# Linear attention and two feed-forward layers in one launch: stores put ahead of loads in the DMA queue, and an attention tile's transpose one step further from its normalisation

## The chip, the cores and the metric

The kernel runs on one core of a Trainium2 chip. The metric is the device time of one execution in microseconds (us); the result quoted for a kernel is the median of several runs. All data is float32; matrix products are made from a high and a low part of each factor, three matmuls for each product.

## The reference

Per batch (8) and head (8), over 576 positions of 64 elements, then over 4608 tokens of 512 elements:

```python
kv  = einsum('bhsd,bhse->bhde', k, v)
o   = einsum('bhsd,bhde->bhse', q, kv)
x   = o / sqrt(mean(o*o, -1) + 1e-6) * g_norm      # laid out as 4608 x 512
h   = x @ w_in1                                    # 512 -> 2048
y   = (h * sigmoid(1.702*h)) @ w_out1              # 2048 -> 512
h2  = y @ w_in2
out = (s * maximum(h2, 0)**2 + b) @ w_out2
```

## The kernel before, in words

**First layer: 144 steps.** Tokens are cut into nine blocks of 512, the 2048 inner features into sixteen groups of 128. A step `n` is one block and one group: `mm1(n)` (L375, 12 matmuls with 512 columns) makes `h`, `act_g`, `act_h` and `act_l` make its activation and its two parts on ScalarE (ACT) and VectorE (DVE), and `mm2(n-2)` (L404, 12 matmuls) adds the group of two steps before to the four sums of the block. Steps 0 to 31 go over blocks 0 and 1 together; from step 32 on, each block has sixteen steps. The loop at L855 writes the order out by hand, and every engine takes its instructions in this order. In each step it runs named slots: `splith`, `mm1`, `norm`, `pe`, `mm2(n-2)`, the copies of a finished block's sums (`y_out`), `act`, `r`, `turn`, `xh`, `xl`, `raw`, `load`, and then two calls of `make`.

**Attention rides along.** For block v (3 and up) with first step n0 = 16(v-1), `kv_at` puts one pair of heads of batch v into each of the steps n0 to n0+3 (`kv_pair` on PE, L223); `load_kv` loads the pair p+2 in the step of pair p, two steps ahead of its use, into buffers `kt` and `vt`. A block has four attention tiles. `tile_at(i, n, n_norm, n_turn)` puts the product `att_u` (PE) with its square `att_sq` (ACT) and row sums `att_r` (DVE, then GpSimd) into step n, the normalisation `att_norm` (DVE, L291) into `n_norm`, and the transposes `att_turn` (PE, L297) with their copies `att_xh`, `att_xl` into `n_turn`. `load_q` loads a tile's q four steps before n.

**Work for the second layer** is done beside the steps 35 to 145, as generators: each call of `make(True)` or `make(False)` advances the first generator of its list to the next `yield`, and goes on to the next generator if that one ends. `prep_in` and `prep_out` split the second layer's weights into parts (an ACT copy L176 or L184, a DVE subtraction L177 or L185) in the one buffer `wst`, which is stored to DRAM. `factors(s)` reads back the first layer's result (`yf`, L342 and L345), adds the parts of blocks 0 and 1 (L349), forms seven combinations (L356 to L359) and stores each as a high and a low part from one of two buffers `xo` (L363, L364).

**One DMA queue.** Every transfer is issued by SyncE (SP), in the order of the program. An instruction that waits holds up all behind it. `move` (L83) issues stores and loads alike; `load_wo` refills, six steps ahead, a ring of eight weight buffers, and waits for the `mm2` that used the buffer last. `load_w` (L108) loads raw weights and waits for the conversion of an earlier one (L134).

**Second layer: 40 pairs.** For each of five couples of blocks and eight pairs of feature groups, seven `product`s (L467) with a Strassen-like scheme are each followed by `after` (L516, on ACT and DVE) and by one or two `units` of the output product (L555). `make(False)` runs what is left of `factors`.

Of the kernel before, what the change touches and what calls it, by code (L numbers as in the profile page):

```python
# [24 lines left out]
TT = BT // P  # L25
# [18 lines left out]
def tile_attn_moe_moe2(  # L44
# [26 lines left out]
    def new(tag, shape=(P, BT), dtype=F32, name=None):  # L71

        return sb.tile(list(shape), dtype, tag=tag, name=name or tag)

    def rot(tag, n, shape=(P, BT), dtype=F32, name=None):

        turns[tag] = turns.get(tag, -1) + 1
        return new(f"{tag}{turns[tag] % n}", shape, dtype, name or tag)

    def move(dst, src):  # L80

        raw = [x.bitcast(F32) if x.dtype == F32R else x for x in (dst, src)]
        nc.sync.dma_start(out=raw[0], in_=raw[1])  # L83
# [94 lines left out]
        move(dst, t)  # L178

    def prep_out(f):  # L180
        w = w_raw.pop((1, 1, f))
        wo_dram[1, f] = dp.tile([P, 2, DM], F32, name=f"wo1_{f}")
        t = new("wst", (P, 2, DM), F32R)
        nc.scalar.copy(t[:, 0, :], w)  # L184
        nc.vector.tensor_tensor(out=t[:, 1, :], in0=w, in1=t[:, 0, :].bitcast(F32), op=ALU.subtract)  # L185
        move(wo_dram[1, f], t)
        yield

    def prep_in(p):
        a, b = (w_raw.pop((0, 1, f)).rearrange("p (h e) -> p h e", h=2) for f in (2 * p, 2 * p + 1))  # L190
# [138 lines left out]
    def factors(s):  # L329


        js = [j for j in (2 * s, 2 * s + 1) if j < NB]
        m = BT * len(js) // 2
        x_dram[s] = [dp.tile([P, 2, 2, m], F32, name=f"x{s}_{i}") for i in range(7)]
        tt = nc.vector.tensor_tensor
        for c in range(2):
            got = {}
            for kk in range(2):
                for n, j in enumerate(js):
                    t = got[kk, n] = new(f"yf{2 * kk + n}")  # L340
                    first, *more = y_dram[j].values()
                    nc.sync.dma_start(out=t, in_=first[2 * kk + c])  # L342
                    others = [new(f"yf{4 + e}") for e, _ in enumerate(more)]
                    for o, part in zip(others, more):
                        nc.sync.dma_start(out=o, in_=part[2 * kk + c])  # L345
                    if others:
                        yield
                    for o in others:
                        tt(out=t, in0=t, in1=o, op=ALU.add)  # L349
            if len(js) == 2:  # L350
                b11, b12, b21, b22 = (got[x] for x in ((0, 0), (0, 1), (1, 0), (1, 1)))
            else:
                (b11, b12), (b21, b22) = ((got[x, 0][:, 0:m], got[x, 0][:, m:]) for x in range(2))
            t1, t2, t4 = (new(f"yf{e}")[:, 0:m] for e in (4, 5, 6))
            yield
            tt(out=t1, in0=b12, in1=b11, op=ALU.subtract)  # L356
            tt(out=t2, in0=b22, in1=t1, op=ALU.subtract)
            tt(out=b12, in0=b22, in1=b12, op=ALU.subtract)
            tt(out=t4, in0=b21, in1=t2, op=ALU.subtract)  # L359
            for i, x in enumerate((b11, b21, t2, t1, b12, b22, t4)):  # L360
                yield
                o = rot("xo", 2, (P, 2, m), F32R)
                nc.scalar.copy(o[:, 0, :], x)  # L363
                tt(out=o[:, 1, :], in0=x, in1=o[:, 0, :].bitcast(F32), op=ALU.subtract)  # L364
                move(x_dram[s][i][:, c], o)
# [9 lines left out]
    def mm1(n, t0=0, t1=BT):  # L375
        v_, f = steps[n][:2]
        wh, wl = w_in[f]
        xh, xl = xT[v_]
        if t0 == 0:
            h_t[n] = bank(f"h{n % 2}", "h")  # L380
        o = h_t[n][:, t0:t1]
        for c in range(KD):
            cs = slice(c * P, (c + 1) * P)
            nc.tensor.matmul(o, wh[:, cs], xh[:, c, t0:t1], start=(c == 0), stop=False)  # L384
            nc.tensor.matmul(o, wl[:, cs], xh[:, c, t0:t1], start=False, stop=False)  # L385
            nc.tensor.matmul(o, wh[:, cs], xl[:, c, t0:t1], start=False, stop=(c == KD - 1))  # L386
# [11 lines left out]
    def act_l(n):  # L398
        gl = gl_t[n] = rot("gl", 2, dtype=F32R)
        nc.vector.tensor_tensor(out=gl, in0=g_t.pop(n), in1=gh_t[n].bitcast(F32), op=ALU.subtract)  # L400
# [213 lines left out]
    def at(n, slot, fn, *args):  # L614
        beside.setdefault((n, slot), []).append((fn, args))

    def run(n, slot):
        for fn, args in beside.pop((n, slot), ()):
            fn(*args)

    def tile_at(i, n, n_norm, n_turn, slot="turn"):

        at(n, "pe", att_u, i)
        at(n, "act", att_sq, i)
        at(n, "r", att_r, i)
        at(n_norm, "norm", att_norm, i)
        at(n_turn, slot, att_turn, i)
        early = "0" if slot == "pe" else ""
        at(n_turn, "xh" + early, att_xh, i)
        at(n_turn, "xl" + early, att_xl, i)  # L630

    def kv_at(bb, p, n):
        at(n, "pe", kv_pair, bb, p)
        if p + 2 < NP:
            at(n, "load", load_kv, bb, p + 2)
        if p == NP - 1:
            at(n, "act", kv_out, bb)
            if bb + 1 < B:
                next_kv(bb + 1, n)
# [19 lines left out]
    n0 = begin[1, CUTS[-2]]  # L659
# [9 lines left out]
    for v_ in range(3, NB):  # L669
        n0 = begin[v_ - 1, 0]  # L670
        if v_ < B:
            for p in range(NP):
                kv_at(v_, p, n0 + p)
        for t in range(TT):
            n = n0 + 4 + 3 * t
            at(n - 4, "load", load_q, v_ * TT + t)
            tile_at(v_ * TT + t, n, n + 1, n + 1)


    def need(w):  # L680
# [36 lines left out]
    with tc.manual_schedule():  # L717
# [131 lines left out]
        def make(weights):  # L849

            got = made[weights]
            while got and next(got[0], got) is got:
                got.popleft()

        for n in range(2, len(steps) + 2):  # L855
            conv = to_f32(*convs.pop(n)) if n in convs else iter(())
            for fn, *args in todo.pop(n, ()):
                made[fn is not factors].append(fn(*args))
            run(n, "splith")
            next(conv, None)  # L860
            if n <= len(steps):
                act_l(n - 1)
            next(conv, None)
            run(n, "splitl")
            next(conv, None)
            if n < len(steps):
                if n > 2:
                    mm1(n)
                act_g(n)
                act_h(n)  # L870
            else:
                for i in (0, 1) if n == len(steps) else (2, 3):
                    product(0, i)
                    after(0, i)
            run(n, "norm")
            run(n, "pe")
            next(conv, None)
            run(n, "xh0")
            run(n, "xl0")
            mm2(n - 2)  # L880
            y_out(n - 2, 0)
            y_out(n - 2, 1)
            run(n, "act")
            run(n, "r")
            next(conv, None)
            y_out(n - 2, 2)
            y_out(n - 2, 3)
            run(n, "turn")
            run(n, "xh")
            run(n, "xl")  # L890
            run(n, "raw")
            run(n, "load")
            make(True)
            make(False)
            if n == NB * KF - 15:
                load_half(0)
                load_half(1)
            if NB * KF - KF < n < NB * KF - 1 and n % 2:
                load_x(0, (n - NB * KF + KF) // 2)
            if n == len(steps):  # L900
                load_half(2)
            if n >= len(steps) - 6 and n % 2:
                load_wo2()
                load_wo2()
# [3 lines left out]
        for P_, (cp, p) in enumerate(pairs):  # L908
            for i in range(4 if P_ == 0 else 0, 7):
                product(P_, i)  # L910
                after(P_, i)
                if i == 2 and P_:
                    running.append(units(P_ - 1))
                for _ in range(2 if i == 6 else 1):
                    while running and next(running[0], StopIteration) is StopIteration:
                        running.pop(0)
                make(False)
                if i == 3 and P_:
                    load_half(2 * P_ + 3)
                if i == 6:  # L920
                    load_half(2 * P_ + 4)
                if cp + 1 < len(couples):
                    if p == 0 and i in (5, 6):
                        load_x(cp + 1, i - 5)
                    if p == KF // 2 - 1 and i < 5:
                        load_x(cp + 1, i + 2)
# [56 lines left out]
```

## Time and profile before

| | us |
|---|---|
| median of 3 runs | 1708.98 (1707.16 to 1713.73) |
| profiled execution, its own time | 1713.6 |
| span of the profiled execution | 1711.8 |
| PE busy | 1639.8 (96%) |
| DVE busy | 911.6 (53%) |
| ACT busy | 667.6 (39%) |

The span is the time from the first to the last instruction of the profile; the execution's own time is 1.8 us longer. A wait is the time in which an engine stood idle before an instruction, put down to the work whose end released it. The 16 DMA engines moved 375.76 MB, 220 GB/s over the span.

### The profile page before, as it was taken

The page shows a single profiled execution, that of the slowest core. Times are in us where ns is not written, and L with a number is a line of the kernel's source. Part 1 is how long each engine was busy: PE and PEld are TensorE (multiplying, and loading weights), DVE is VectorE, ACT ScalarE, POOL GpSimd, SP SyncE. Part 2 cuts the span into 40 slices and gives each one's busy share as a digit, 9 for nine tenths or more (in the row PEclk, how much of TensorE's full clock was granted, in tenths as well). Part 3 has the DMA queues.
Part 4 walks back from the last instruction along what each step waited for, and adds up shares of the span by engine and source line. Part 5 has one row for each costly group of instructions (what it writes and reads, how often), then busy time and mean ns, then how long its engine had stood idle before and what let it go on. Part 6 is the DMA issues. An engine that isn't in the chain of part 4 may idle for free.

```text
span 1711.8 us, 21305 instructions
## 1 busy us (share of the span) xinstructions
PE 1639.8 (96%) x7996; PEld 1354.3 (79%) x7996; DVE 911.6 (53%) x1512; ACT 667.6 (39%) x1161; POOL 75.1 (4%) x52
## 2 busy tenths in 40 slices
PE   8899999989979999999999799999999999999998
PEld 6687887767867878777888688888888888888887
DVE  5876637565446544665544455554454454555443
ACT  4565633434334433443333343333334333333333
POOL 3200101000000000000000000000000000000000
PEclk9999999989989999999999999999999999999999
DMA  6566757686566845767478964684377447644773
GB/s 222 168 220 202 265 203 273 244 294 222 197 227 241 311 161 185 265 226 265 148 273 299 319 234 135 224 286 142 135 262 252 139 148 263 208 136 148 245 277 118
DMA packets 125239, 375.76 MB, mean 220 GB/s; under 512 B 14416, under 2 KB 18000, under 8 KB 119632
## 3 DMA queue, kind: packets, MB, share of 16 engines
q1 hardware_dynamic: 125136, 374.40, 63.1%
q8 instruction: 63, 1.03, 0.2%
q14 instruction: 40, 0.33, 0.1%
HBM read 284.69 MB, written 89.65 MB: 219 GB/s over the span
## 4 chain that ended last, share of the span: by engine, by line
PE 77%; DMA 10%; DVE 7%; ACT 2%; issue 2%; SPq 1%; POOL 0%; ACTq 0%; DVEq 0%; POOLq 0%
PE h L384 6%; PE h L385 6%; PE h L386 6%; PE acc L413 5%; PE acc L414 5%; PE acc L415 5%; DMA wi<-wst 4%; PE sum L575 4%; PE sum L576 4%; PE sum L577 4%; PE A L480 4%; PE A L482 4%; PE A L481 4%; PE z L575 3%; PE z L576 3%; PE z L577 3%
## 5 line engine op out<-in xcount | busy, mean ns | idle before, releaser
L384 PE MATMUL h<-xh,wih 128*128 128x512 f32 (+1 forms) x580 | 234.2, 404 | 0.0
L413 PE MATMUL acc<-gh,wo 128*128 128x512 f32 x576 | 230.6, 400 | 3.4 <-DVE xl L318 3.4
L385 PE MATMUL h<-xh,wil 128*128 128x512 f32 (+1 forms) x580 | 230.5, 397 | 0.0
L386 PE MATMUL h<-xl,wih 128*128 128x512 f32 (+1 forms) x580 | 230.2, 397 | 0.2 <-DVE xl L318 0.2
L414 PE MATMUL acc<-gh,wo 128*128 128x512 f32 x576 | 225.7, 392 | 1.3 <-DVE wo L150 1.3
L415 PE MATMUL acc<-gl,wo 128*128 128x512 f32 x576 | 225.7, 392 | 1.0 <-DVE gl L400 1.0
L391 ACT ACTIVATE g<-h 128x512 f32<-128x512 f32 x144 | 86.0, 597 | 254.0 <-PE h L386 253.7
L392 DVE TENSOR_TENSOR g<-g,h 128x512 f32<-128x512 f32 x144 | 98.6, 685 | 148.2 <-ACT g L391 148.0
L396 ACT CAST gh<-g 128x512 fp32r<-128x512 f32 x144 | 89.5, 621 | 172.3 <-DVE g L392 172.3
L386 PEld LDWEIGHTS h<-xl,wih 128*128 128x128 f32 x580 | 112.3, 194 | 24.5 <-DVE xl L318 0.4
L385 PEld LDWEIGHTS h<-xh,wil 128*128 128x128 f32 x580 | 112.7, 194 | 22.6
L384 PEld LDWEIGHTS h<-xh,wih 128*128 128x128 f32 x580 | 112.5, 194 | 22.6
L413 PEld LDWEIGHTS acc<-gh,wo 128*128 128x128 f32 x576 | 108.9, 189 | 26.8 <-DVE xl L318 3.6
L415 PEld LDWEIGHTS acc<-gl,wo 128*128 128x128 f32 x576 | 108.7, 189 | 24.4 <-DVE gl L400 1.4
L414 PEld LDWEIGHTS acc<-gh,wo 128*128 128x128 f32 x576 | 108.9, 189 | 23.1 <-DVE wo L150 2.0
L400 DVE TENSOR_TENSOR gl<-g,gh 128x512 fp32r<-128x512 f32 x144 | 99.9, 694 | 26.4 <-PE acc L415 24.6
L287 POOL TENSOR_TENSOR r<-ms,mhalf 128x8 f32<-128x8 f32 x36 | 65.4, 1823 | 752.6 <-DVE ms L286 752.6
L480 PE MATMUL A<-wih,xl 128*128 128x512 f32 (+1 forms) x212 | 79.0, 373 | 7.6 <-ACT gh L544 7.6
L524 DVE TENSOR_TENSOR wst<-B,wst 128x512 f32<-128x512 f32 (+1 forms) x40 | 25.5, 638 | 99.2 <-PE B L482 99.2
L481 PE MATMUL A<-wih,xl 128*128 128x512 f32 (+1 forms) x212 | 78.3, 369 | 0.0
L482 PE MATMUL A<-wil,xl 128*128 128x512 f32 (+1 forms) x212 | 78.2, 369 | 0.0
L585 DVE TENSOR_TENSOR g<-z,g 128x512 f32<-128x512 f32 x56 | 38.7, 691 | 55.8 <-PE z L577 55.5
(236 smaller groups left out, 3146.2 us busy)
## 6 DMA issues: line engine op xcount, KB each, us to landing
wo<-wo SPq DMA_DIRECT2D x208, 512.0 KB, 4.6
x<-xo SPq DMA_DIRECT2D x56, 512.0 KB, 5.2
xl<-wi SPq DMA_DIRECT2D x26, 1024.0 KB, 5.3
xl<-wi SPq DMA_DIRECT2D x27, 768.0 KB, 4.4
wraw<-in_w_in SPq DMA_DIRECT2D x32, 512.0 KB, 3.6
wraw<-in_w_out SPq DMA_DIRECT2D x32, 512.0 KB, 3.5
y<-ev SPq DMA_DIRECT2D x60, 256.0 KB, 2.9
yf<-y SPq DMA_DIRECT2D x60, 256.0 KB, 5.2
```

The lines of the kernel that those rows point to most:

```text
L384: nc.tensor.matmul(o, wh[:, cs], xh[:, c, t0:t1], start=(c == 0), stop=False)
L385: nc.tensor.matmul(o, wl[:, cs], xh[:, c, t0:t1], start=False, stop=False)
L386: nc.tensor.matmul(o, wh[:, cs], xl[:, c, t0:t1], start=False, stop=(c == KD - 1))
L413: nc.tensor.matmul(o, wh[:, ds_], gh, start=(f == lo), stop=False)
L414: nc.tensor.matmul(o, wl[:, ds_], gh, start=False, stop=False)
L415: nc.tensor.matmul(o, wh[:, ds_], gl, start=False, stop=(f == hi - 1))
L480: nc.tensor.matmul(o, wh, xh, start=(c == 0 and not more), stop=False, skip_group_check=more)
L481: nc.tensor.matmul(o, wl, xh, start=False, stop=False, skip_group_check=more)
L482: nc.tensor.matmul(o, wh, xl, start=False, stop=(c == 1), skip_group_check=more)
L575: nc.tensor.matmul(o, gh[:, cs], wh, start=begins, stop=False)
L576: nc.tensor.matmul(o, gh[:, cs], wl, start=False, stop=False)
L577: nc.tensor.matmul(o, gl[:, cs], wh, start=False, stop=ends)
```

## The change

`prep_out` yields before its work and not behind it. `factors` yields once more after it has added the parts of blocks 0 and 1. For blocks 3 to 8 an attention tile's product and normalisation come one step earlier (n0+3+3t and n0+4+3t) and its transposes stay where they were (n0+5+3t); its q is loaded one step earlier too. In the steps of the first layer `make` runs ahead of the slots `raw` and `load`, so that the stores and the reads of `prep_in`, `prep_out` and `factors` come ahead of that step's loads in SP's queue. In the second layer `make(False)` runs after products 1 and 4 of a pair and not after each of the seven.

```diff
     def prep_out(f):
+        yield
         w = w_raw.pop((1, 1, f))
...
         move(wo_dram[1, f], t)
-        yield
...
                     for o in others:
                         tt(out=t, in0=t, in1=o, op=ALU.add)
+                    if others:
+                        yield
...
         for t in range(TT):
-            n = n0 + 4 + 3 * t
+            n = n0 + 3 + 3 * t
             at(n - 4, "load", load_q, v_ * TT + t)
-            tile_at(v_ * TT + t, n, n + 1, n + 1)
+            tile_at(v_ * TT + t, n, n + 1, n + 2)
...
             run(n, "xl")
+
+            make(True)
+            make(False)
             run(n, "raw")
             run(n, "load")
-            make(True)
-            make(False)
...
-                make(False)
+                if i in (1, 4):
+                    make(False)
```

## Rows read from the trace of the kernel before

**Rows 1.** The page: TensorE clock granted in 40 slices of the span, in tenths.

```profile
PEclk9999999989989999999999999999999999999999
```

**Rows 2.** Busy time by stage: window, length, busy time (x instructions) of each engine, clock, DMA.

```profile
256.00:944.00 688.00, 650.57 (x3202) 533.23 (x3201) 369.38 (x634) 253.38 (x445) 43.95 (x24) 0.97 0.68 240
944.00:1003.00 59.00, 49.12 (x195) 38.92 (x194) 29.56 (x52) 22.21 (x41) 0.00 (x0) 0.91 0.84 294
1003.00:1626.00 623.00, 623.00 (x2778) 517.10 (x2777) 318.29 (x472) 224.08 (x364) 0.00 (x0) 1.00 0.57 196
```

**Rows 3.** Waits of PE from 256 to 944 us: total, times, longest.

```profile
PE xtp L297 <- ACT gh L396: 21.2, 4, 10.9
PE xtp L297 <- DVE xn L291: 15.2, 7, 3.4
```

**Rows 4.** The longest wait of PE from 944 to 1003 us.

```profile
PE A L480 <- ACT gh L544: 5.5, 1, 5.5
```

**Rows 5.** Busy time of four steps: a stalled transposing step and its next, two unstalled ones.

```profile
474.12:491.34 17.22, 6.33 (x30) 5.09 (x28) 6.29 (x11) 2.84 (x5) 1.95 (x1) 0.81 0.88 305
491.34:498.64 7.30, 7.30 (x26) 5.88 (x25) 4.51 (x8) 4.05 (x7) 0.00 (x0) 0.74 0.17 72
504.99:510.79 5.80, 5.80 (x30) 4.82 (x28) 2.52 (x5) 1.22 (x2) 1.95 (x1) 1.00 0.69 247
510.79:516.36 5.57, 5.57 (x27) 4.59 (x26) 4.50 (x8) 4.04 (x7) 0.00 (x0) 1.00 0.51 188
```

**Rows 6.** Timeline of DVE: start, length, instruction, idle time before it and its releaser.

```profile
485.17 0.69 DVE L356 TENSOR_TENSOR yf<-yf,yf 128x512 f32<-128x512 f32 x1 [7.93 <-DMA yf<-y]
...
488.57 0.68 DVE L400 TENSOR_TENSOR gl<-g,gh 128x512 fp32r<-128x512 f32 x1
...
489.77 0.68 DVE L291 TENSOR_TENSOR xn<-u,r 128x512 f32<-128x512 f32 x1
```

**Rows 7.** Timeline of SP's queue in the same stretch.

```profile
469.95 0.32 SPq L83 DMA_DIRECT2D wo<-wst  x1
473.31 0.33 SPq L108 DMA_DIRECT2D wraw<-in_w_in  x1
...
477.89 2.33 SPq L342 DMA_DIRECT2D yf<-y  x4
```

**Rows 8.** Timeline of PE: another stalled transpose.

```profile
376.83 1.08 PE L297 MATMUL xtp<-ident,xn 128*128 128x128 f32 x4 [7.75 <-ACT gh L396]
```

**Rows 9.** Timeline of SP's queue before it.

```profile
364.09 0.33 SPq L83 DMA_DIRECT2D wo<-wo  x1
364.70 0.33 SPq L83 DMA_DIRECT2D wi<-wst  x1
```

**Rows 10.** Timeline of ACT in the same stretch.

```profile
371.01 0.62 ACT L176 CAST wst<-wc 128x512 fp32r<-128x512 f32 x1 [3.04 <-DMA wi<-wst]
```

**Rows 11.** Timeline of ACT at the start of the second layer.

```profile
963.11 0.62 ACT L363 CAST xo<-yf 128x512 fp32r<-128x512 f32 x1 [2.40 <-DMA x<-xo]
...
972.23 0.41 ACT L363 CAST xo<-yf 128x256 fp32r<-128x256 f32 x1 [4.39 <-DMA yf<-y]
```

**Rows 12.** The tile wst, 250 to 900 us: from the issue of a store to its landing.

```profile
DMA to landing us min/median/max: 2.0/3.7/8.3
```

**Rows 13.** Timeline of SP's queue: the load of batch 4's last pair of v.

```profile
348.77 0.50 SPq L218 DMA_DIRECT2D vt<-in_v  x1
```

**Rows 14.** The tile vt, 345 to 360 us: from issue to landing.

```profile
DMA to landing us min/median/max: 4.6/4.6/4.6
```

**Rows 15.** Timeline of PE: the product that uses it.

```profile
353.54 0.69 PE L237 MATMUL kvps<-vt,kt 128*64 128x64 f32 x16
```

**Rows 16.** The same for batch 5: SP's queue, 453 to 458 us.

```profile
456.76 0.60 SPq L218 DMA_DIRECT2D vt<-in_v  x1
```

**Rows 17.** The tile vt, 455 to 465 us: from issue to landing.

```profile
DMA to landing us min/median/max: 6.2/6.2/6.2
```

**Rows 18.** Timeline of PE: the product that uses that load.

```profile
464.18 0.69 PE L237 MATMUL kvps<-vt,kt 128*64 128x64 f32 x16
```

## The prediction

> **What bounds the kernel now.** The first view is the page. TensorE (PE) is busy 96% of the span, and the granted clock stands at nine tenths or more in all slices but two [rows 1]. So nothing can be won on PE's work, which the change leaves as it is; what can be won is PE's idle time and the time in which its clock is down. The busy time by stage says where that lies. From 1003 to 1626 us PE has no gap and full clock: 2778 matmuls in 623 us, 4.459 a microsecond. From 256 to 944 us it is busy 650.57 of 688.00 us at a mean clock of 0.97, and from 944 to 1003 us 49.12 of 59.00 us at 0.91 [rows 2]. The waits of PE name the causes. In the first stretch 21.2 + 15.2 us of the 37.4 us idle stand before the transposes of attention tiles (L297); a single wait of 1.0 us is somewhere else [rows 3]. In the second stretch products wait for ACT to empty a sum, 5.5 us the first and longest time [rows 4].
>
> **What a stall costs beside itself.** A step whose transposes wait, from the start of its mm1 to that of the next, took 17.22 us and the step behind it 7.30 us; an unstalled couple took 5.80 and 5.57 us [rows 5]. The excess is 13.15 us, of which 10.89 us is PE's idle time (17.22 less 6.33), so 2.26 us is matmuls at a low clock: the granted clock was 0.74 in the step behind the stall, a mixture of the levels 1.2 and 2.4 GHz, after PE had stood still. Eight of the twelve waits in this stretch are longer than 1.5 us (10.9 us the longest [rows 3]), and each is followed by such a slow spell; behind the four shorter ones the timeline has none. 8 x 2.26 = 18.1 us. The mean clock of 0.97 over 688 us says 20.6 us, so the two agree roughly [rows 2].
>
> **The ceiling of the gain.** From 256 to 944 us: 37.4 + 18.1 = 55.5 us. From 944 to 1003 us: at 4.459 a microsecond 59.00 us hold 263.1 matmuls, and 195 were made, so 68.1 x 0.224 us = 15.3 us are lost, idle time and clock together. In all 70.8 us. The profiled execution's own time was 1713.6 us, so with all of this gone it is 1642.8 us. Before 256 and behind 1003 us the change touches nothing that PE waits for. The median shown, 1709.0 us, is 4.6 us below this execution; I don't take that off, because what differs between executions is most likely the stalls, and without them both end at the same place.
>
> **Two steps between product and transpose.** Where the largest stall ended, DVE had stood 7.93 us for a read of yf; then came the four combinations, the low part gl at 488.57 us, and the normalisation at 489.77 us, 0.68 us long, for which the transposes waited [rows 6]. With the transposes a step later PE goes on with the next mm1: twelve matmuls, 2.7 us. Then it comes to the mm2 that needs this very gl, ready at 489.25 us. The normalisation ended at 490.45 us and PE had then waited 10.9 us [rows 3], from 479.6 us on; it would stop again at 482.3 us and wait 7.0 us. So this part alone takes 3.9 us from a stall: the waits for DVE of at most 3.4 us [rows 3] go entirely, that of 10.9 us becomes 7.0 us, and one of 7.75 us [rows 8] 3.8 us. The other two of the four put down to ACT share 2.55 us (21.2 - 10.9 - 7.75) and go too. The moved instructions cost nothing: product, square and row sums fall into the step before, where they lie beside the step's 24 matmuls; in each block's fourth step they share PE with a kv_pair, and the same matmuls are missing one step later. The product's bank comes free in the step behind its own, as before; the transposes use the other one of the two banks. The q load moves one step earlier with its product and stays four steps ahead.
>
> **Stores and reads ahead of loads.** For the 10.9 us: the yf reads were issued at 477.89 us, behind a raw weight load that had waited for DVE until 473.31 us and eight other loads. The last store before them was issued at 469.95 us [rows 7]. Behind that store alone, the reads go out near 470.3 us, 7.6 us earlier; DVE's 7.93 us become about 0.3 us, and what was left of this stall goes. For the 7.75 us: a wst store was issued at 364.70 us behind the ring's refill at 364.09 us, which waits for PE's mm2 [rows 9]; the next ACT copy into the single buffer waited 3.04 us for its landing [rows 10], and DVE, the combinations and the normalisation came behind it. With the store ahead, most of the 3.04 us goes and so do the remaining 3.8 us. The extra yields (eight, in factors(0) alone; sixteen prep_outs a step later) move work of 0.4 to 0.7 us a piece into steps where DVE has room: it is busy 369 of 688 us [rows 2]. They lengthen factors(0) from 24 to 32 calls, which still end where factors(1) begins; nothing reads the result before step 129.
>
> What is put behind the stores is late by what they take: ring refills and raw loads have six steps in hand, some 33 us, and can bear that. The kv loads have two steps, and are the tight place. The last pair of batch 4 is issued at 348.77 us [rows 13], lands 4.6 us later [rows 14], and its product starts at 353.54 us [rows 15]: 0.17 us in hand. For batch 5 it is 456.76 us [rows 16] plus 6.2 us [rows 17] against 464.18 us [rows 18]: 1.2 us. Ahead of the first there is now an xo store, ahead of the second a wst store and an xo store, 512 KB each; at the 305 GB/s of the fullest step shown [rows 5] that is 1.7 us a store. Lower bound 0: the yf reads that filled the queue just before go away from there, and DVE is no longer late. Upper bound, with 1.4 us more for SP's wait on DVE (two operations of 0.7 us) and batch 6 taken as batch 5: 2.9 + 3.6 + 3.6 = 10.1 us, and three slow spells, 6.8 us: 16.9 us. I take 3 us, nearer the lower end, because the queue is emptier there than before.
>
> **make(False) at two of seven products.** ACT stood 2.40 us for the landing of an xo store and 4.39 us for a yf read [rows 11], and the copies that free PE's banks were queued behind it [rows 4]. Now a call comes every three or four products, some 9 us apart, longer than either needs; the seventeen calls left end some nine pairs in, and the fifth couple needs them in pair 31. Of the 15.3 us I leave 2 us standing.
>
> **Sum.** 1642.8 + 3 (kv loads) + 2 (second layer's start) + 2 (DVE and ACT late now and then in the first) = 1650 us.
>
> **Rivals.** Kv loads late: the stores' bytes and SP's wait at the upper bound in three blocks, 1650 - 3 + 16.9 = 1664 us. For it speak margins of 0.17 and 1.2 us, against it the reads that leave the queue. The Trainium skill (DMA: Bandwidth & Descriptors, Queues, rings and completion order) says that each DMA engine takes the descriptors of one queue in ring order, so that a load behind two stores starts behind their bytes; by that this rival holds in full, and no run here shows yet how much of it does.
>
> The low part takes the transpose's place: the queue's part brings nothing, gl stays late, and PE waits 7.0 + 3.8 us with two slow spells of 2.26 us, 15.3 us instead of 2: 1663 us. Against it: the rows name SP's order as the cause of both.
>
> The second layer's start stays as it is, since ACT is late there for another reason: 1650 - 2 + 15.3 = 1663 us.
>
> The other side: wst is one buffer, and now five users follow each other step by step, eight times. One turn is 0.62 us (ACT), 0.69 us (DVE), 0.33 us (issue) and the landing, 3.7 us in the median and 8.3 us at most [rows 6, 7, 10, 12]: 5.3 us against a step of about 5.7 us. If every landing took 8.3 us, a turn would be 9.9 us, ACT would fall 4.2 x 5 = 21.2 us behind in each group, and less one step of slack that is 15.5 x 8 = 124 us: 1774 us. It decides from the landing at which 8 x (5 x (L + 1.64 - 5.7) - 5.7) reaches the 63.6 us of the gain, L = 6.8 us; the median is far from that.
>
> **How the numbers follow.** Forecast 0.60, kv loads 0.16, gl 0.13, second layer's start 0.05, wst 0.03, and 0.03 that losses I don't see eat the gain up. A measurement of this kernel tells changes over about 0.5% (8.5 us) from none. The forecast and the first three rivals are faster by 45 us or more: 0.94; no change 0.03; slower 0.03. The range goes from just below the ceiling's 1642.8 us to the three rivals at 1663 and 1664 us, which it holds in part.
>
> **What would show it.** Right: from 256 to 944 us no wait of PE before L297 over 1 us, granted clock 1.00, DVE's wait for yf before L356 and ACT's for wst near 0, xo stores and yf reads ahead of the refill in SP's queue; from 944 us on no wait before L480. Wrong: waits before L237 (kv loads), before L415 (gl), or ACT at L176 and L184 behind the landing of wst in every step.

## The result and the profile after

| | us |
|---|---|
| before, median | 1710.68 (1707.16 to 1713.73) |
| after, median | 1656.53 (1655.56 to 1658.53) |
| ratio | 0.9686, 95% interval 0.9663 to 0.9709 |
| profiled execution of after: own time, span | 1656.05, 1654.2 |
| predicted | 1650 (1642 to 1664) |

The page of the kernel after, clock granted in 40 slices, which answers to [rows 1]:

```profile
PEclk9899999999999999999999999999999999999999
```

The busy time by stage; the columns are those of [rows 2]. The second layer's first product stands at 892.88 us here and stood at 943.67 us before, so the stages are cut there:

```profile
256.00:892.80 636.80, 634.76 (x3210) 524.11 (x3209) 368.65 (x632) 252.83 (x445) 43.63 (x23) 1.00 0.73 259
892.80:950.00 57.20, 52.64 (x218) 42.62 (x217) 29.79 (x47) 21.57 (x38) 0.00 (x0) 0.94 0.79 284
...
1003.00:1570.00 567.00, 567.00 (x2533) 470.67 (x2532) 289.93 (x432) 204.10 (x333) 0.00 (x0) 1.00 0.59 203
```

In the first layer PE now misses 2.04 us of 636.80 where it missed 37.43 us of 688.00 us before [rows 2], and its granted clock is 1.00. At the second layer's start 4.56 us are still idle and the clock is 0.94. The waits of PE of the kernel after, 256 to 1000 us, where [rows 3, 4] stood before. The line numbers of this kernel have moved by one to three: L343 and L359 to L362 here are L342 and L356 to L359 of before, L403 is L400, L483 is L480:

```profile
PE A L483 <- ACT gh L547: 2.5, 1, 2.5
PE z L578 <- DVE g L585: 2.1, 1, 2.1
PE kvps L237 <- DMA vt<-in_v: 2.0, 2, 1.4
```

No line of a transpose (L297) is left. Two of the three lines are new: kv products that wait for their load, and a product of the output units (z) that waits for DVE; before, one such product waited 0.4 us, just behind this stretch.

SP's queue of the kernel after, in the step in which factors(1) begins, as in [rows 7]:

```profile
450.05 0.32 SPq L83 DMA_DIRECT2D wo<-wst  x1
450.65 0.32 SPq L83 DMA_DIRECT2D x<-xo  x1
451.02 2.93 SPq L343 DMA_DIRECT2D yf<-y  x4
454.00 0.43 SPq L108 DMA_DIRECT2D wraw<-in_w_in  x1
```

The reads of yf stand behind two stores only, and the raw load and the eight others behind them. DVE in the same stretch, as in [rows 6]:

```profile
453.18 0.68 DVE L291 TENSOR_TENSOR xn<-u,r 128x512 f32<-128x512 f32 x1
455.87 0.69 DVE L359 TENSOR_TENSOR yf<-yf,yf 128x512 f32<-128x512 f32 x1 [2.01 <-DMA yf<-y]
458.28 0.69 DVE L360 TENSOR_TENSOR yf<-yf,yf 128x512 f32<-128x512 f32 x1 [1.71 <-DMA yf<-y]
...
460.09 0.68 DVE L403 TENSOR_TENSOR gl<-g,gh 128x512 fp32r<-128x512 f32 x1
```

The wait of 7.93 us has become 2.01 + 1.71 us, and the normalisation of this tile (L291) now stands ahead of it. ACT's waits for the buffer wst, 256 to 900 us, are one line, of 28.2 + 24.6 us in two before:

```profile
ACT wst L176 <- DMA wi<-wst: 11.1, 4, 3.6
```

### The profile page after: what moved, and what is told of

The parts are those of the page before. It is cut to its first block, busy times and chain, and to the rows that moved or that the text cites. A ratio compares the mean times of both kernels' runs of the same rounds, so it can differ in the third digit from the quotient of the medians.

```text
span 1654.2 us, 21293 instructions
## 1 busy us (share of the span) xinstructions
PE 1621.3 (98%) x7996; PEld 1343.6 (81%) x7996; DVE 911.6 (55%) x1512; ACT 665.8 (40%) x1161; POOL 75.6 (5%) x52
## 4 chain that ended last, share of the span: by engine, by line
PE 93%; DMA 3%; DVE 2%; ACT 1%; issue 1%; SPq 0%; ACTq 0%; DVEq 0%
PE acc L416 8%; PE acc L418 8%; PE acc L417 8%; PE h L387 8%; PE h L389 8%; PE h L388 8%; PE sum L578 4%; PE sum L579 4%; PE sum L580 4%; PE A L483 4%; PE A L484 4%; PE A L485 4%; PE z L578 3%; PE z L579 3%; PE z L580 3%; PE D L485 2%
## 5 line engine op out<-in xcount | busy, mean ns | idle before, releaser
L387 PE MATMUL h<-xh,wih 128*128 128x512 f32 (+1 forms) x580 | 228.6, 394 | 0.0
L389 PE MATMUL h<-xl,wih 128*128 128x512 f32 (+1 forms) x580 | 225.7, 389 | 0.2 <-DVE xl L318 0.2
L388 PE MATMUL h<-xh,wil 128*128 128x512 f32 (+1 forms) x580 | 225.6, 389 | 0.0
L403 DVE TENSOR_TENSOR gl<-g,gh 128x512 fp32r<-128x512 f32 x144 | 99.9, 694 | 28.5 <-PE acc L418 26.8
L483 PE MATMUL A<-wih,xl 128*128 128x512 f32 (+1 forms) x212 | 79.3, 374 | 4.6 <-ACT gh L547 4.6
```

What stands on the lines that cost most here:

```text
L483: nc.tensor.matmul(o, wh, xh, start=(c == 0 and not more), stop=False, skip_group_check=more)
```

## Experiments

The ratios are to the kernel before on the same chip. The medians of before were 1709.85 us for the first four and 1709.97 us for the last four.

**Spacing alone.**

```diff
-            n = n0 + 4 + 3 * t
+            n = n0 + 3 + 3 * t
...
-            tile_at(v_ * TT + t, n, n + 1, n + 1)
+            tile_at(v_ * TT + t, n, n + 1, n + 2)
```

> The kernel before with the attention tiles' new spacing alone (product and normalisation a step earlier, transposes where they were). My theory: SP's queue makes DVE and ACT late, and the spacing only gives one step of slack; no wait before the transposes L297, but PE waits for the low part gl in mm2 for about 7.0 and 3.8 us; idle time of PE from 256 us to the first product of the second layer about 11 us (37.4 before), with two slow spells; gain about 40 us, ratio 0.977; the second layer's start unchanged. Rival 'spacing does it all': idle time there under 2 us, gain 53 us or more, ratio 0.969. Rival 'queue order does it all': the waits only move to mm2, gain under 10 us, ratio above 0.994.

1682.72 us, ratio 0.984 (0.9814 to 0.9865). Waits of PE in this kernel, 255 to 1010 us, and then the longest on PE's timeline:

```profile
PE acc L415 <- DVE gl L400: 15.3, 5, 7.5
...
PE kvps L237 <- DMA vt<-in_v: 2.6, 3, 1.8
```

```profile
477.93 0.79 PE L415 MATMUL acc<-gl,wo 128*128 128x512 f32 x1 [7.47 <-DVE gl L400]
```

Every wait before L297 is gone, and mm2 waits for the low part instead, 7.5 us where 7.0 was worked out. The second, of 7.75 us before, left 2.0 us where 3.8 was worked out. DVE and ACT are as late as ever: ACT waits 30.8 + 27.7 us for wst. So the spacing shifts the limit by one step and removes no cause. Both rivals fall. The size was too high: 27 us were won and not 40. PE idles 17.9 us from 256 to 900 us and not 11, since three more waits for gl (2.5, 1.9 and 1.4 us) and three for kv loads were not in the estimate. Another 3.8 us is that the estimate started from the profiled execution of before, 1713.6 us, and the ratio from the median, 1709.85 us. The kv loads wait although nothing was put ahead of them; the likely reason is that PE is earlier and SP's queue is not, which no run tests.

**Queue order alone.**

```diff
+            make(True)
+            make(False)
             run(n, "raw")
             run(n, "load")
-            make(True)
-            make(False)
```

> The kernel before with the calls of make ahead of the slots raw and load, alone. My theory: the waits of 7.75 and 10.88 us go, because DVE's wait for yf and ACT's for wst fall; short waits before L297 (1 to 3 us each) stay where ACT still waits for the one wst buffer; idle time of PE in the first layer from 256 us on about 10 us; gain about 36 us, ratio 0.979. Rival 'queue order does it all': idle time under 3 us, gain 50 us, ratio 0.970. Rival 'spacing does it all': the long waits stay, gain under 10 us.

1681.48 us, ratio 0.9835 (0.9813 to 0.9857). The waits of PE in this kernel, 255 to 1010 us, and below them those of ACT for wst, 255 to 920 us:

```profile
PE xtp L297 <- DVE xn L291: 11.4, 8, 3.1
...
PE kvps L237 <- DMA vt<-in_v: 4.5, 2, 4.1
```

```profile
ACT wst L184 <- DMA wi<-wst: 27.3, 8, 4.4
ACT wst L176 <- DMA wi<-wst: 5.6, 3, 4.0
```

The two long waits are gone and 11.4 us of short ones stay, as my theory had it; both rivals fall. The gain was too high again, 28.4 us and not 36: PE idles 16.3 us from 256 to 900 us where about 10 was expected. What I had not put in is the kv load of 4.1 us: the next four reads of yf now stand ahead of it. At L184, where two users of wst meet in one step, the order of the queue helps nothing (27.3 us, 28.2 before); at L176 it takes 24.6 to 5.6 us.

**Queue order and yields.** As the last, and

```diff
     def prep_out(f):
+        yield
...
-        yield
...
                         tt(out=t, in0=t, in1=o, op=ALU.add)
+                    if others:
+                        yield
```

> As e2, with the yields moved and added too (prep_out a step later, factors once more after adding the parts), spacing as before. My theory: two users of wst no longer meet in one step, so ACT's wait at L184 falls below 3 us in total (28.2 us before) and 2 to 5 us more than in e2 are won: ratio about 0.977. If the yields do nothing by themselves it equals e2 within 2 us.

1673.96 us, ratio 0.9789 (0.9769 to 0.9809): 7.5 us less than the queue order alone. The same two views of this kernel:

```profile
PE xtp L297 <- DVE xn L291: 7.0, 3, 4.0
...
PE kvps L237 <- DMA vt<-in_v: 1.7, 1, 1.7
```

```profile
ACT wst L176 <- DMA wi<-wst: 12.5, 6, 3.7
```

L184 no longer waits, and the kv load waits 1.7 us and not 4.5 us: the extra yield in factors spreads the reads of yf over twice as many steps. The yields carry more than was expected of them (2 to 5 us). Both were moved in one run, so how the 7.5 us divide between them is not shown.

**Calls in the second layer alone.**

```diff
-                make(False)
+                if i in (1, 4):
+                    make(False)
```

> The kernel before with make(False) after products 1 and 4 of a pair alone. It touches the second layer only. My theory, as the trace after left it: the waits 5.5, 1.2, 2.7 and 0.4 us before products fall to about 4.6 us in two places (2.5 us before L480 in the first pair, 2.1 us behind a late yf read), gain 7 us, ratio 0.996. As the prediction had it: gain 13 us, ratio 0.992. Rival 'ACT is late there for its own work': gain under 3 us.

1703.71 us, ratio 0.9965 (0.995 to 0.998): 6.1 us less. The waits of PE in this kernel at the second layer's start:

```profile
PE z L575 <- DVE g L582: 3.8, 1, 3.8
PE A L480 <- ACT gh L544: 2.5, 1, 2.5
```

Four waits, 9.9 us, become two, 6.3 us. So the prediction's 13 us for this part fall, and so does the rival, which had under 3 us.

**The kernel after again**, to stand beside the next three.

> The kernel after itself, to stand beside the next three on the same chip: 1656 us, ratio 0.969, with waits of PE of about 2.0 us before the kv products L237 and 4.6 us at the second layer's start.

1657.00 us, ratio 0.9705 (0.9681 to 0.9729). All waits of PE of this execution, 255 to 1010 us:

```profile
PE z L578 <- DVE g L585: 3.6, 1, 3.6
PE kvps L237 <- DMA vt<-in_v: 2.7, 3, 1.4
PE A L483 <- ACT gh L547: 2.5, 1, 2.5
```

The same three lines; the wait before the z unit differs from one execution to the other (2.1 and 3.6 us), and the kv products wait three times and not twice.

**Kv loads ahead of make.**

```diff
-            at(n, "load", load_kv, bb, p + 2)
+            at(n, "kv", load_kv, bb, p + 2)
...
             run(n, "xl")
+            run(n, "kv")
             make(True)
             make(False)
```

> The kernel after with the loads of kt and vt of the pair p+2 in a slot of their own ahead of the calls of make, so that no store of that step stands before them in SP's queue. My theory: the two waits before L237 (1.40 and 0.63 us) came from the stores' bytes and from SP's wait for DVE, and go; 2 us less than the kernel after, ratio to before 0.967. Rival: the load is late for the finished block's four stores that stand ahead of it in either order; the waits stay within 0.5 us of what they were.

1654.92 us, ratio 0.9685 (0.9661 to 0.971): 2.1 us less than the kernel after. Its waits of PE have no line of L237 left; a single wait of 0.5 us for gl came up. The rival, that the finished block's own stores make the load late, falls. SP's queue with the load of batch 5's last pair, and its landing:

```profile
431.81 2.51 SPq L429 DMA_DIRECT2D y<-ev  x4
434.40 1.06 SPq L218 DMA_DIRECT2D kt<-in_k  x1
435.52 0.72 SPq L218 DMA_DIRECT2D vt<-in_v  x1
```

```profile
DMA to landing us min/median/max: 4.5/4.5/4.5
```

The four stores of the finished block end at 434.32 us, and the load of vt is issued 1.2 us later.

**One call a pair.**

```diff
-                if i in (1, 4):
+                if i == 1:
                     make(False)
```

> The kernel after with make(False) after product 1 of a pair alone, from the second pair on. My theory: the wait of 2.1 us before L578 came from a yf read that was needed 4.5 us after its issue and landed after 8.9 us; with a whole pair (20 us) between the calls it goes with its slow spell, 3.5 us; the 2.5 us before L483 are the chain of ACT and DVE in a first pair that has no units beside its products, and stay but for some 0.6 us of a cast that leaves it. 3.5 to 4 us less than the kernel after, ratio to before 0.9665. Rival: the second wait is that chain too, and stays: no change within 1 us.

1649.94 us, ratio 0.9661 (0.9637 to 0.9685): 7.1 us less than the kernel after. All waits of PE in this kernel, 255 to 1010 us:

```profile
PE kvps L237 <- DMA vt<-in_v: 2.4, 2, 1.5
PE A L483 <- ACT gh L547: 1.3, 1, 1.3
```

The wait before the z unit is gone, so it was the read; the rival falls. More was won than the 3.5 to 4 us expected: that wait was 3.6 us in the kernel after beside it, with a slow spell behind it, and the one before L483 fell by 1.2 us and not by 0.6.

**Both.** The two edits together.

> Both edits of the two runs before on the kernel after. If the two causes are separate their gains add: 5 to 6 us less than the kernel after, near 1650.5 us, ratio to before 0.965, with one wait of PE of 2 us from 256 us to the last couple. If not, it equals the better of the two.

1647.76 us, ratio 0.9643 (0.9617 to 0.967): 9.2 us less than the kernel after, which is the sum of 2.1 and 7.1. More was won than the 5 to 6 us expected, because one call a pair had brought 7.1 us. The two causes are separate, and this version beats both kernels. Its waits of PE from 255 to 1010 us, in full, and its busy time in the first layer's stage:

```profile
PE A L483 <- ACT gh L547: 1.3, 1, 1.3
```

```profile
256.00:892.80 636.80, 636.80 (x3218) 525.53 (x3218) 369.95 (x634) 252.33 (x446) 43.44 (x24) 1.00 0.74 260
```

## Why the prediction was right, and where its sum was off

**The ceiling and its place.** Right. The gain lies where the trace showed idle time and slow clock. From the first product of the second layer back to step 34, the first layer's stage is 53.1 us shorter (705.4 us before, from 238.31 to 943.67 us; 652.2 us after, from 240.66 to 892.88 us); 55.5 us were put down to it, and 2.0 us of new waits are in the stage.

**Two steps between product and transpose.** Right in mechanism and nearly in size: alone it turned the wait of 10.9 us into 7.5 us before L415 (7.0 worked out). In the whole change no wait for gl is left in the trace, so the 2 us left standing for late DVE and ACT were not needed.

**Stores and reads ahead of loads.** Right in mechanism: alone it removed both long waits. It did not bring the waits for landings to near zero, as the prediction said it would show: DVE's wait for the first reads of factors(1) is 3.7 us and not 0.3 us, and ACT waits 11.1 us for wst. The sum had the reads 7.6 us earlier, behind one store; in the kernel after they stand behind two, go out at 451.02 us, and DVE is ready for them 2.8 us later, at 453.86 us, less than the 4.8 us after which the first two had landed. These waits cost PE nothing, because the spacing stands behind them; without it, with queue order and yields alone, 7.0 us of waits for DVE before L297 are left. The extra yields, which the prediction costed at nothing, are a part of their own: 7.5 us between the two experiments, seen at L184 and at the kv loads.

The parts overlap. Alone, spacing gives 27 us, queue and yields 36 us, the calls 6 us, together 69 us; all at once they give 53 us. A stall that either the slack or the cause takes away is counted twice.

**Kv loads.** The new wait is real and at the place that was named. Three views of the kernel after: SP's queue with the load of batch 5's last pair, the landing of that load (the tile vt), and PE's timeline with its product:

```profile
432.86 2.52 SPq L429 DMA_DIRECT2D y<-ev  x4
435.48 0.85 SPq L83 DMA_DIRECT2D wi<-wst  x1
436.42 0.67 SPq L83 DMA_DIRECT2D x<-xo  x1
437.18 0.89 SPq L218 DMA_DIRECT2D kt<-in_k  x1
438.12 1.13 SPq L218 DMA_DIRECT2D vt<-in_v  x1
```

```profile
DMA to landing us min/median/max: 6.3/6.3/6.3
```

```profile
444.54 0.69 PE L237 MATMUL kvps<-vt,kt 128*64 128x64 f32 x16 [1.40 <-DMA vt<-in_v]
```

A wst store and an xo store stand ahead of it; it lands at 444.4 us, and PE waits 1.40 us, in batch 6 0.63 us: 2.0 us against the 3 us taken, and far from the rival's 16.9 us. The batch with 0.17 us in hand does not wait here: as said, the reads that filled the queue ahead of it are gone from there. In the second execution of this kernel it waited 0.36 us. Loads ahead of make took the waits away, which shows the cause, and the two traces part what the two stores cost. Behind them vt is issued 2.7 us after the end of the block's stores (435.38 us), ahead of them 1.2 us: 1.5 us of SP's issue, with no wait for DVE of more than 0.1 us in it. Behind them it lands after 6.3 us, ahead of them after 4.5 us (batch 6: 5.9 and 4.7 us): 1.8 us and 1.2 us longer behind both stores together, where the prediction took 1.7 us for the bytes of each. By the ring order that the Trainium skill states (DMA: Bandwidth & Descriptors, Queues, rings and completion order) a load starts behind the stores that stand ahead of it; the longer landings behind the stores (6.3 us against 4.5 us) agree.

**make(False) at two of seven products.** This is the term that was mis-sized. At the rate of 1003 to 1570 us, 2533 / 567 = 4.467 matmuls a microsecond, the 57.20 us of the stage hold 255.5, and 218 were made: 37.5 x 0.224 = 8.4 us are left, where the prediction left 2 us. The step that failed is that a call every three or four products, "some 9 us apart", is longer than either landing needs. The timelines of SP's queue and of DVE in the kernel after show it:

```profile
918.15 0.91 SPq L343 DMA_DIRECT2D yf<-y  x2
```

```profile
921.99 0.69 DVE L538 TENSOR_TENSOR wc<-A,wc 128x512 f32<-128x512 f32 x1 [0.74 <-PE A L485]
927.03 0.42 DVE L359 TENSOR_TENSOR yf<-yf 128x256 f32<-128x256 f32 x1 [4.35 <-DMA yf<-y]
```

The reads were issued at 918.15 us, behind an xo store that was itself late; DVE was ready for them at 922.68 us, 4.5 us later; and they took 8.9 us to land, with loads of a megabyte ahead. The rest of the term is the wait of 2.5 us before L483. It halved when the cast of xo left the first pair. That what remains, 1.3 us, is the chain of ACT and DVE in a first pair that has no output units between its products is argued from the timeline, not shown.

**The sum again with what was measured.** 1642.8 + 2.0 (kv) + 0 + 8.4 (second layer's start) = 1653.2 us; the profiled execution took 1656.05 us. That the forecast of 1650 us came this near is in part luck: the second layer's start cost 6.4 us more than was left for it, and the 2 us for DVE and ACT and 1 us of the kv loads were not used. Most of the rest lies ahead of 256 us, nearly all of it ahead of the first work that the change touches. The same stretch before, after, and with the calls in the second layer alone, whose first layer is that of before:

```profile
0.00:256.00 256.00, 239.10 (x1366) 197.08 (x1367) 161.54 (x281) 135.14 (x238) 31.12 (x28) 0.99 0.64 213
```

```profile
0.00:256.00 256.00, 237.44 (x1356) 195.72 (x1357) 160.73 (x282) 134.41 (x236) 32.01 (x29) 0.97 0.63 213
```

```profile
0.00:256.00 256.00, 238.39 (x1359) 196.14 (x1360) 160.03 (x280) 134.41 (x236) 30.39 (x28) 0.97 0.63 212
```

Ten matmuls fewer are 2.2 us at the rate above; the clock is 0.97 and not 0.99. Step 34 begins 2.35 us later. With the unchanged first layer the clock is 0.97 as well and step 34 begins 1.4 us later than before (239.72 us), so at least the larger part is a difference between executions and not of the change. Where it comes from is open.

**The rivals.** That gl takes the transpose's place is what the spacing does alone; the queue's part prevents it. The wst rival falls: the landing of a wst store went from 3.7 us in the median to 2.9 us, away from the 6.8 us from which it would decide. The second layer's start did not stay as it was either: 8.4 us of 15.3 us are left.

## What to carry to other kernels

When an in-order engine waits for a landing, look at what stood ahead of the transfer in the issuing queue, and at whether that waited for something which the transfer doesn't need; then give the consumer a step of slack as well, since each alone took away only half to two thirds of what all parts together did. What is put behind moved stores needs its own margin worked out, load by load: here the sum named the place of the only new wait, and one line more in the queue's order removed it. The distance between a read and its use is to be taken between their positions on the engines, with the landing that the queue has at that place, not from a count of products and a median.

## What the runs showed of the hardware

The landing time of one and the same kind of transfer moved with its place in the queue: the last load of vt of a batch from 6.3 and 5.9 us behind two stores of 512 KB to 4.5 and 4.7 us ahead of them, wst stores from a median of 3.7 us to 2.9 us, reads of yf from 255 to 1000 us from a median of 5.1 us and 7.9 us at most to a median of 4.4 us and 9.6 us at most.

A low clock doesn't follow from the length of the wait alone. With the spacing alone, the granted clock was 0.50 (the level of 1.2 GHz, matmuls 0.43 us apart) for 3.3 us behind a wait of PE of 1.92 us, and 1.00 behind waits of 1.99 and 2.51 us; in the kernel after it was 0.50 behind 2.10 and 2.46 us, and 1.00 behind 1.40 us. One and the same wait shows it best: 2.46 us before L483, in the two executions of the kernel after, the first with a slow spell behind it and the second without:

```profile
910.50:913.80 3.30, 3.30 (x8) 2.65 (x9) 2.96 (x5) 1.69 (x3) 0.00 (x0) 0.50 1.00 317
```

```profile
909.90:914.00 4.10, 4.10 (x18) 3.19 (x19) 3.62 (x6) 2.15 (x4) 0.00 (x0) 1.00 0.98 354
```
